# Theta's whole turns taken off by TensorE for the first two units, and a new order of steps

## The chip, the cores and the metric

The kernel runs on one core of a Trainium2 chip, in one launch. The metric is the time of one execution on the device, in microseconds, as the median of several runs; of the kernel before there are three, from 584.65 to 585.68, with a median of 585.23.

## The reference

Three stages over B = 4 batches of S = 768 tokens and 8 heads of 48 channels (384 together); all is float32.

```python
state = zeros((B, H, D, D))
for t in range(S):                       # 1: attention with a decaying state
    state = alpha[:, :, t, :, None] * state + einsum('bhd,bhe->bhde', k[:, :, t], v[:, :, t])
    y[:, :, t] = einsum('bhd,bhde->bhe', q[:, :, t], state)
x = y as (B, S, 384)
theta = x @ w_theta                      # 2: first mixer
z = einsum('ts,bsd->btd', w_tok_r, x * cos(theta)) + einsum('ts,bsd->btd', w_tok_i, x * sin(theta))
u = x + z
x = u + maximum(u @ w_ch, 0)
h = maximum(x @ w_in, 0); u, v = halves of h      # 3: second mixer, d_ff = 1024
v_n = (v - mean(v)) / sqrt(var(v) + 1e-6)
out = (u * (einsum('ts,bsd->btd', w_spatial, v_n) + b_spatial)) @ w_out
```

## The kernel before, in words

**Units.** The first two stages run over 24 units: unit u is batch u // 6 and a block of 128 tokens, u % 6. A unit's work is cut into steps, each a small function that issues its instructions on one engine:

- loads on SP's queue: load_al, load_qk, load_v; load_cst once (identity and mask)
- attention: att_scan (VectorE, three instructions: running products of the decays), att_qk (VectorE, q and k times the decays), att_a (TensorE, scores), att_mask for two halves (VectorE), move_a (SP: one half of the masked scores moved to the other partitions, through a tile "ay"), att_k (TensorE, four transposes of k), att_kt (ScalarE copies them), att_u (TensorE, update of the state), att_t and att_s (VectorE: state summed, then decayed, for two chunks c), att_y (TensorE, output), att_x (ScalarE copies it to x). From unit 6 on att_uy does att_u of the next unit and att_y together.
- first mixer: tr_p (TensorE, three transposes of x), tr_t and tr_h (ScalarE copies), tr_l (VectorE, the rest that tr_h's rounding leaves), th_p part 0 (six products with w_theta) and part 1 (three), th_k (ScalarE: theta in turns plus a magic constant, which rounds it to whole turns), th_r (VectorE: whole turns minus theta, into r), th_a (ScalarE: absolute value), th_s 0 and 1 (ScalarE: cosine and sine), z_m (VectorE: x times both), z_h and z_l (ScalarE, VectorE: split in two parts), tokmix for three blocks m and two of cos/sin (TensorE). Unit 0 is mixed in plain fp32 from whole tiles (line 610, tiles wf and zs), all others in three fp32r products of split parts.
- at a batch's end evac, ch_h, ch_l, ch_p, ch_e, ch_d: the channel product and the store of x to DRAM.

**Weights.** They come as 64-bit pieces: raw_f64 n loads one piece (on POOL's queue for n < 16, on SP's beyond) into one of two raw buffers, top n (ScalarE) and join n (VectorE) make a float32 of it, high n (ScalarE) and low n (VectorE) split that into two fp32r parts. Pieces 0 and 1 are w_theta, 2 to 13 the token weights, 14 and 15 w_ch. A load waits until join has read the buffer.

**The second mixer** runs batch by batch behind this: v_p, v_r, v_b, v_w, v_n, v_h, v_l; g_u and g_r; for batch 0 g_s, for the others seven block products g_p; g_b or g_c, g_m, g_h, g_l; o_p, o_e, o_d.

**Order.** Every step is registered once, with its engine and what it needs, and then issued in the order of the list ORDER (line 78 on), which holds the steps' numbers. Each engine executes its own steps in that order, as does SP's queue, so a step that waits holds up all behind it on its engine. The fields of `step` (cost, due time) play no part in the execution.

**Buffers that matter here.** PSUM has five accumulator banks and a pool "ps" of three banks. Theta of a unit (tile th), the transposes, the outputs y, and from unit 3 on the scores and k take turns in that pool. The SBUF buffers: al two, qk three, vd two (load_v), raw two.

**Lines named in the rows:** 342 load_al, 347 load_qk, 352 load_v, 357 to 361 att_scan, 369 att_qk, 383 att_a, 391 att_mask, 401 move_a, 407 att_k, 424 att_u, 434 att_s, 447 att_t, 466 att_y, 239 top, 248 join, 259 high, 267 low, 494 tr_p, 501 tr_h, 519 tr_l, 534 and 537 th_p, 541 th_k, 551 th_r, 572 z_m of unit 0, 610 tokmix.

Of the kernel before, what the change touches and what calls it, by code (L numbers as in the profile page):

```python
# [62 lines left out]
THP = ()  # L63
# [15 lines left out]
129 0 163 130 164 66 131 6 165 132 133 67 138 68 134 139 167 166 11 69 140 7 141 70 202 135 8 137 168 1 9 203 136 12 142 169 10 176 173 13 170 16 174  # L79
205 143 172 175 144 2 145 177 171 178 147 3 240 241 179 36 4 204 206 180 146 148 5 17 211 214 18 149 212 243 21 181 207 37 150 244 182 151 213 183 208  # L80
184 209 249 210 152 185 153 186 215 242 155 38 154 187 250 216 41 156 39 278 245 22 217 157 40 188 247 23 161 252 24 26 246 189 248 218 25 190 192 159
279 281 191 280 219 42 251 220 160 222 253 43 193 162 76 44 254 221 45 316 27 224 317 255 194 223 28 225 256 282 29 31 158 257 195 77 30 226 283 227
198 78 230 284 46 228 319 258 286 196 260 259 318 79 200 287 199 288 261 80 32 290 289 285 320 229 201 14 291 231 325 262 33 232 292 326 71 263 233
353 34 197 391 293 264 35 47 321 265 238 323 266 328 268 322 294 15 267 324 269 327 295 355 239 48 354 270 329 296 49 51 271 236 298 297 72 300 330 50
299 390 19 73 331 356 56 74 301 392 332 276 333 277 334 75 302 335 237 303 336 304 357 337 52 306 234 53 393 61 358 338 274 339 305 235 360 340 394
362 341 272 54 359 363 307 361 57 395 20 273 308 465 55 275 397 309 364 396 343 365 399 58 342 427 314 400 366 59 344 367 62 60 310 401 428 368 63 398
315 402 64 403 430 464 345 369 81 312 370 429 371 91 373 372 313 346 374 65 311 375 431 349 404 376 432 467 379 350 377 378 436 351 437 433 1015 405
435 468 347 406 466 434 380 82 407 348 438 408 439 409 440 381 473 410 501 352 441 474 502 1014 411 382 469 389 1016 412 383 470 413 414 385 504 415
417 442 1017 387 443 503 471 505 539 472 384 475 476 510 477 444 511 478 538 388 1018 446 445 416 386 447 83 506 1019 512 86 508 418 507 419 448 1020
509 420 479 541 421 575 480 540 423 513 514 449 515 574 425 542 450 1021 549 451 452 481 1022 424 482 453 484 483 543 454 1023 544 545 546 455 485 577  # L90
456 422 486 547 1024 487 426 548 1025 488 457 489 516 1026 578 462 576 517 1027 611 518 583 550 520 463 551 584 610 491 460 519 490 521 579 458 581
492 552 580 493 613 582 522 553 612 648 459 585 586 647 523 494 1030 524 525 614 526 461 528 527 619 529 499 620 554 555 530 557 1031 556 495 1032 650
558 1028 496 1029 1033 559 531 1034 615 560 497 617 561 651 562 587 563 616 564 621 500 588 649 565 685 622 589 566 532 623 624 684 591 658 590 618
656 592 593 657 652 536 653 654 655 687 498 594 625 595 567 534 722 626 659 596 533 660 721 661 627 688 686 535 628 597 630 629 631 695 599 598 693
570 724 694 689 632 571 633 691 634 537 690 635 600 87 662 725 601 568 602 723 663 692 696 664 569 697 665 795 698 666 1037 637 572 636 1036 726 667
573 727 609 729 728 668 638 758 605 639 640 730 603 731 1038 699 761 1039 606 760 759 669 732 607 670 700 671 604 674 733 734 701 735 794 608 1040 702
703 672 705 673 675 645 704 676 1043 762 797 767 768 646 706 707 1045 1044 708 677 709 1041 769 710 711 682 1042 712 763 713 641 765 764 714 766 736
798 643 1046 737 770 738 771 683 740 830 739 796 1048 799 801 741 1047 831 642 800 1049 802 719 833 644 803 742 804 678 772 743 832 868 720 744 773
745 679 748 805 834 867 746 1052 747 749 774 806 680 750 1053 776 835 775 681 777 751 778 837 836 870 838 839 779 756 780 840 1050 781 784 782 807
1051 783 785 1054 808 905 869 841 842 843 809 1055 717 904 810 871 1056 786 715 844 878 812 813 787 718 907 814 876 815 754 877 811 716 908 845 816  # L100
752 906 846 942 817 879 755 880 818 881 941 819 872 847 820 849 757 874 821 848 822 753 873 851 850 875 944 790 909 852 911 791 853 854 913 910 855
792 915 912 914 1059 882 945 788 883 979 916 884 917 789 885 918 978 886 887 857 793 1058 946 829 888 947 1060 949 950 825 981 943 889 823 890 856 827
891 951 858 892 1061 824 982 859 860 919 828 826 1062 980 920 948 861 84 85 921 862 923 952 922 893 953 865 924 894 954 955 983 895 925 984 896 985 88
863 89 101 926 864 92 90 927 897 987 1067 93 989 102 104 928 898 1068 988 931 103 866 107 1063 105 902 929 106 930 900 1064 110 932 986 899 933 956
934 1065 957 990 991 958 903 960 959 111 961 962 112 901 1066 113 963 1069 937 964 965 992 966 108 939 993 109 1070 1109 935 96 1071 994 114 940 995
115 967 1072 968 116 969 1074 1073 970 996 971 1076 1075 998 1077 997 1078 936 999 938 1000 1001 976 1002 1003 1035 972 974 1004 117 1005 118 1006 977
97 119 1007 975 94 1012 95 98 973 1112 124 1010 1114 1113 1013 1008 1081 1011 1115 1009 1080 1057 1116 1079 1091 1082 1123 1092 1117 1118 1097 1124
1119 99 1125 1093 1100 1083 1126 1130 1120 1098 1121 100 1095 1094 1122 1084 1127 1131 1101 1128 1088 120 1085 1096 1129 1086 1099 1132 1106 1089 1133
1087 1104 1107 1090 121 1102 1134 122 1105 125 1110 1137 123 1135 126 1136 1181 127 1138 1139 1144 1103 1140 1108 1141 128 1160 1145 1142 1146 1214
1111 1151 1161 1234 1147 1224 1148 1143 1149 1158 1152 1153 1167 1159 1150 1154 1155 1156 1174 1157 1162 1235 1236 1238 1169 1163 1164 1215 1165 1168  # L110
1237 1195 1216 1170 1166 1171 1176 1225 1175 1220 1226 1218 1188 1177 1178 1182 1183 1228 1179 1172 1180 1244 1229 1202 1184 1245 1190 1185 1186 1230
# [13 lines left out]
1580 1582 1581 1619 1583 1592 1620 1648 1585 1593 1586 1625 1641 1594 1595 1587 1596 1588 1589 1626 1590 1597 1621 1598 1655 1601 1649 1602 1599 1675  # L125
1600 1622 1623 1657 1624 1643 1627 1632 1659 1633 1628 1629 1636 1644 1660 1642 1630 1645 1650 1631 1646 1668 1651 1647 1637 1634 1656 1652 1661 1635
1658 1638 1639 1666 1653 1640 1676 1662 1654 1677 1667 1663 1664 1670 1669 1665 1678 1679 1684 1671 1680 1672 1682 1673 1674 1685 1689 1681 1683 1686
1687 1688 1692 1690 1691 1695 1693 1694 1698 1696 1697 1701 1699 1700 1704 1702 1703 1705 1706
""".split()]


# [1304 lines left out]
```

## Time and profile before

| | |
|---|---|
| median of three runs | 585.23 us |
| the profiled execution | 585.29 us |
| its span | 583.5 us |
| TensorE busy | 561.5 us, 96% |
| VectorE busy | 440.3 us, 75% |
| ScalarE busy | 252.5 us, 43% |
| GpSimd busy | 25.1 us, 4% |
| moved by DMA | 66.23 MB |

The span runs from the first to the last instruction of the program. In the rows PE is TensorE, DVE is VectorE, ACT is ScalarE, POOL is GpSimd and SP is SyncE, which issues most loads and stores; L551 is line 551 of the kernel. A row in order of time begins with the start and the duration in us; a number in brackets at its end is the engine's idle time before the instruction, and what ended it. An fp32 matmul shows as two records. Matmuls are pipelined: a duration reaches into that of the next one, so what a step costs is read from the distance of starts, or from a merged row of several.

### The profile page before, as it was taken

What the parts mean: (1) busy time and instruction counts of PE and PEld (TensorE: products, weight loads), DVE (VectorE), ACT (ScalarE), POOL (GpSimd) and SP (SyncE); (2) the same over time, 40 slices, a digit from 0 to 9 for tenths busy, and PEclk for the clock granted to TensorE, in tenths of its full rate; (3) what the DMA queues carried; (4) which work ended last, traced back from release to release, by engine and by line L of the source; (5) the groups of instructions that cost most, each with busy time, mean ns of one, the idle gap of its engine ahead of it and who ended that gap; (6) DMA issues with size and microseconds to landing.
All of it is one profiled execution on the core that took longest, in us unless ns stands there. A gap on an engine that the chain in (4) does not pass through costs nothing.

```text
span 583.5 us, 13445 instructions
## 1 busy us (share of the span) xinstructions
PE 561.5 (96%) x5737; PEld 510.4 (87%) x5737; DVE 440.3 (75%) x769; ACT 252.5 (43%) x474; POOL 25.1 (4%) x45
## 2 busy tenths in 40 slices
PE   1799999999999999999999999999999999999997
PEld 1666878888988889988989899999999899989997
DVE  6999999988788876878756887776665775767470
ACT  2476755435335433334554443534323441343232
POOL 1101100000000000000000100000000100011000
PEclk9999999999999999999999999999999999999999
DMA  8878756363253324333344525001002010211002
GB/s 287 295 240 278 245 184 215 112 198 126 86 169 110 104 88 128 122 104 97 95 139 168 180 89 183 1 0 62 20 2 95 29 41 0 82 42 40 1 1 81
DMA packets 28220, 66.23 MB, mean 114 GB/s; under 512 B 3073, under 2 KB 14337, under 8 KB 27905
## 3 DMA queue, kind: packets, MB, share of 16 engines
q1 hardware_dynamic: 25984, 53.51, 27.7%
q0 software_dynamic: 2176, 11.86, 5.9%
q8 instruction: 45, 0.74, 0.5%
q14 instruction: 15, 0.11, 0.1%
HBM read 52.78 MB, written 9.44 MB: 107 GB/s over the span
## 4 chain that ended last, share of the span: by engine, by line
PE 79%; DVE 10%; DMA 4%; ACT 2%; issue 2%; POOL 1%; DVEq 0%; SPq 0%; POOLq 0%; ACTq 0%
PE acc L610 22%; PE acc L929 11%; PE pu L861 8%; PE psc L652 7%; PE po L987 7%; PE psv L788 6%; PE sp L900 4%; PE th L534 3%; PE psuy L466 3%; DMA raw<-in_w 3%; PE th L537 2%; PE psa L383 2%; PE psuy L424 2%; PE psk L407 1%; DVE wf L248 1%
## 5 line engine op out<-in xcount | busy, mean ns | idle before, releaser
L610 PE MATMUL acc<-w,zs 128*128 128x256 f32 (+1 forms) x828 | 165.2, 344 | 0.0
L610 PEld LDWEIGHTS acc<-w,zs 128*128 128x128 f32 x828 | 128.0, 188 | 15.4
L788 PE MATMUL psv<-w,xs 128*128 128x512 f32 x216 | 53.7, 395 | 0.0
L987 PE MATMUL po<-w,gs 128*128 128x384 f32 x288 | 52.8, 338 | 0.3 <-ACT v L799 0.3
L861 PE MATMUL pu<-xs,w 128*128 128x384 f32 x288 | 53.0, 336 | 0.0
L987 PEld LDWEIGHTS po<-w,gs 128*128 128x128 f32 x288 | 50.7, 188 | 1.6 <-ACT v L799 0.7
L861 PEld LDWEIGHTS pu<-xs,w 128*128 128x128 f32 x288 | 50.3, 188 | 0.7 <-ACT o L997 0.2
L788 PEld LDWEIGHTS psv<-w,xs 128*128 128x128 f32 x216 | 40.0, 187 | 8.2 <-ACT v L799 0.2
L652 PE MATMUL psc<-us,wch 128*128 128x384 f32 (+1 forms) x243 | 41.2, 320 | 0.0
L652 PEld LDWEIGHTS psc<-us,wch 128*128 128x128 f32 x243 | 37.8, 189 | 0.8
L541 ACT ACTIVATE kk<-th,magic 128x384 f32<-128x384 f32 x24 | 13.9, 578 | 53.3 <-PE th L537 53.3
L973 ACT CAST gs<-t 128x384 fp32r<-128x384 f32 x32 | 15.8, 513 | 48.3 <-DVE t L966 48.3
L811 POOL TENSOR_TENSOR rs<-rs,mhalf 128x1 f32<-128x1 f32 x24 | 15.6, 652 | 441.7 <-DVE rs L808 441.7
L357 DVE TENSOR_TENSOR_SCAN al<-al,heads 112x536 f32<-112x536 f32 x24 | 30.5, 1270 | 3.3 <-DMA al<-in_al 3.3
L534 PE MATMUL th<-wth,xh 128*128 128x384 f32 x144 | 31.1, 352 | 0.9 <-ACT xh L501 0.5
L361 DVE TENSOR_TENSOR_SCAN al<-al,heads 112x536 f32<-112x536 f32 x24 | 30.6, 1275 | 0.8
L369 DVE TENSOR_TENSOR qk<-qk,al 112x1024 f32<-112x1024 f32 x24 | 29.3, 1220 | 2.1 <-DMA qk<-in_qk 2.1
L929 PE MATMUL acc<-w,mx 128*128 128x384 f32 x162 | 30.7, 338 | 0.0
L929 PE MATMUL acc<-wt,vns 128*128 128x384 f32 x162 | 30.7, 338 | 0.0
L929 PEld LDWEIGHTS acc<-wt,vns 128*128 128x128 f32 x162 | 28.6, 188 | 0.1
L929 PEld LDWEIGHTS acc<-w,mx 128*128 128x128 f32 x162 | 28.6, 188 | 0.0
L534 PEld LDWEIGHTS th<-wth,xh 128*128 128x128 f32 x144 | 25.4, 194 | 2.6 <-ACT xh L501 2.0
(122 smaller groups left out, 977.5 us busy)
## 6 DMA issues: line engine op xcount, KB each, us to landing
qk<-in_qk SPq DMA_DIRECT2D x24, 512.0 KB, 4.7
raw<-in_w POOLq DMA_DIRECT2D x14, 772.0 KB, 6.4
vd<-in_v SPq DMA_DIRECT2D x24, 288.0 KB, 4.0
al<-in_al SPq DMA_DIRECT2D x24, 268.0 KB, 3.3
raw<-in_w SPq DMA_DIRECT2D x6, 772.0 KB, 5.5
out<-o SPq DMA_DIRECT2D x24, 192.0 KB, 1.8
x2d<-xT SPq DMA_DIRECT2D x6, 576.0 KB, 4.4
ay<-ax SPq DMA_DIRECT2D x48, 64.0 KB, 2.8
```

Source lines behind the costliest of these rows:

```text
L357: nc.vector.tensor_tensor_scan(out=back[:, ::-1], data0=line[:, ::-1], data1=one[:, ::-1], initial=1.0, op0=ALU.mult, op1=ALU.add)
L361: nc.vector.tensor_tensor_scan(out=line, data0=line, data1=one, initial=0.0, op0=ALU.mult, op1=ALU.add)
L369: nc.vector.tensor_tensor(out=x, in0=x, in1=st[u]["ar"], op=ALU.mult)
L466: nc.tensor.matmul(psy[par][64 * c:64 * c + 64, a, :], w, v, start=part == 0 or first, stop=part == 1,)
L534: nc.tensor.matmul(th, xh[:, 0, k], wth[:, pr, k], start=(k == 0 and pr == 0), stop=False)
L610: nc.tensor.matmul(acc[b, n][:, c0:c1], zs[:, pl, ri, m * 128:(m + 1) * 128], w[:, pr, t0:t1], start=first and n != 1, stop=last, skip_gro ...
L652: nc.tensor.matmul(ps, wch[:, pl, k, m * 128:(m + 1) * 128], us[:, pr, k], start=(n == 0), stop=(n == 3 * KD - 1),)
L788: nc.tensor.matmul(ps, xs2[:, pl, k, o:o + 128], win[pr, "v"][:, k], start=(n == 0), stop=(n == 3 * KD - 1),)
L861: nc.tensor.matmul(pu, win[f // 2][:, pl, k * 256 + f % 2 * 128:k * 256 + f % 2 * 128 + 128], xq[b, h][:, pr, k], start=(n == 0), stop=(n ...
L900: nc.tensor.matmul(sp[:, :TH], vns[b, s][:, pl, f * 128:(f + 1) * 128], wsp[s][:, pr, t], start=(n == 0), stop=(n == 3 * NS - 1),)
L929: nc.tensor.matmul(g, left(b, n, j, pl, c), right(n, j, pr), start=(n in (1, 5, 6) and i == 0), stop=(i == 3 * NJ - 1), skip_group_check=n ...
L987: nc.tensor.matmul(po, gs[b][:, pl, f, s * 128:(s + 1) * 128], wo[f // 2][:, pr, f % 2 * DM:(f % 2 + 1) * DM], start=(n == 0), stop=(n == ...
```

## The change

One setting and the order differ.

THP = (0, 1) instead of an empty tuple. With it, for units 0 and 1, th_r goes, and two steps stand in its place: th_n (ScalarE) takes the magic constant off kk, which leaves the whole turns, and th_m (TensorE) multiplies them by a negative identity and adds that to theta in its PSUM bank. th_a and th_s 1 then read theta from that bank, not r. A step negate (ScalarE) makes the negative identity, 128x128, from the identity of load_cst. The functions were in the kernel before, unused.

```diff
-THP = ()
+THP = (0,1)
 STP = ()
...
-129 0 163 130 164 66 131 6 165 132 133 67 138 68 134 139 167 166 11 69 140 7 141 70 202 135 8 137 168 1 9 203 136 12 142 169 10 176 173 13 170 16 174
...
+130 131 67 165 166 7 0 132 167 168 133 134 68 135 69 169 12 8 139 70 140 141 137 136 71 138 142 170 205 206 9 171 143 2 10 178 13 11 175 173 1 172 14
...
```

The whole list is replaced; as the new steps are numbered in between, equal numbers don't mean equal steps. Decoded, by engine, the first steps read (unit or piece behind the name; att_mask, att_s, att_t with unit and half or chunk; th_p with unit and part; tokmix with unit, m and cos/sin):

```
PE before: att_k 0, att_a 0, att_u 0, att_a 1, att_k 1, att_y 0, att_u 1, tr_p 0, att_y 1, att_k 2, th_p 0 0, att_a 2, th_p 0 1, tr_p 1,
  att_u 2, att_k 3, th_p 1 0, th_p 1 1, att_a 3, tokmix 0 0 0, tokmix 0 2 0, att_y 2, tokmix 0 1 0, att_u 3, tr_p 2
PE after:  att_a 0, att_k 0, att_u 0, att_a 1, att_k 1, att_u 1, att_y 0, tr_p 0, att_y 1, att_k 2, th_p 0 0, th_p 0 1, tr_p 1, att_a 2,
  att_u 2, th_m 0, att_k 3, th_p 1 0, th_p 1 1, att_a 3, tokmix 0 0 0, th_m 1, att_y 2, tokmix 0 1 0, att_u 3, tokmix 0 2 0, tr_p 2
DVE before: att_scan 0, att_qk 0, join 13, att_scan 1, att_s 0 1, low 13, att_mask 0 0, join 1, att_qk 1, att_mask 0 1, att_t 0 1, low 1,
  att_s 1 0, join 2, att_mask 1 0, att_scan 2, att_t 1 0, att_mask 1 1, att_s 1 1, join 0, att_t 1 1, att_qk 2, tr_l 0, low 0, att_s 2 0,
  join 3, att_scan 3, att_qk 3, att_mask 2 0, att_mask 2 1, th_r 0, tr_l 1, att_t 2 0, join 7, att_s 2 1, z_m 0
DVE after: att_scan 0, att_qk 0, join 13, att_scan 1, att_mask 0 1, att_mask 0 0, low 13, att_s 0 1, att_qk 1, join 1, att_t 0 1, att_s 1 0,
  low 1, att_mask 1 1, att_mask 1 0, join 2, att_scan 2, att_t 1 0, att_s 1 1, att_qk 2, join 0, att_t 1 1, tr_l 0, att_s 2 0, low 0,
  join 3, att_scan 3, att_qk 3, tr_l 1, att_t 2 0, att_mask 2 0, att_s 2 1, join 7, z_m 0
ACT before: top 13, att_kt 0, high 13, top 1, high 1, top 2, att_kt 1, att_x 0, top 0, tr_t 0, high 0, tr_h 0, top 3, att_kt 2, att_x 1,
  top 7, th_k 0, tr_h 1, tr_t 1, th_a 0, th_s 0 1, th_s 0 0, att_kt 3
ACT after: top 13, top 1, high 13, att_kt 0, high 1, top 2, negate, att_kt 1, att_x 0, top 0, tr_h 0, tr_t 0, high 0, top 3, att_x 1, att_kt 2,
  th_k 0, tr_t 1, th_n 0, tr_h 1, top 7, th_a 0, th_s 0 1, th_s 0 0, att_kt 3
SP before: al 0, cst, qk 0, al 1, v 0, qk 1, v 1, al 2, move_a 0, qk 2, move_a 1, al 3, qk 3, v 2, move_a 2, v 3
SP after:  al 0, qk 0, al 1, cst, v 0, qk 1, v 1, move_a 0, al 2, qk 2, move_a 1, v 2, al 3, qk 3, v 3, move_a 2
```

POOL's queue of weight loads is the same in both (13, 1, 2, 0, 3, 7, 4, 8, 5, 15, 6, 9, 14, 10, 11, 12). Further on the same kind of changes goes through the whole list: token mixes of neighbouring units change places, some loads (qk 6, v 7, al 9, pieces 16 and 18) move by a few places in SP's queue, and in the second mixer some g_u, g_p, o_p and v_p change places. VectorE executes the same steps up to z_l 6, but for th_r 0 and 1. The last four steps of TensorE are the same.

## Rows read from the trace of the kernel before

**Rows 1.** The page, engines: busy us, share, instructions.
```profile
PE 561.5 (96%) x5737; PEld 510.4 (87%) x5737; DVE 440.3 (75%) x769; ACT 252.5 (43%) x474; POOL 25.1 (4%) x45
```

**Rows 2.** Windows: stretch, length, busy by engine (instructions), PEclk, DMA share, GB/s.
```profile
0.00:20.00 20.00, 5.72 (x110) 4.69 (x110) 15.41 (x27) 6.37 (x9) 3.70 (x10) 1.00 0.81 276
20.00:40.00 20.00, 17.80 (x280) 14.20 (x283) 18.41 (x32) 12.18 (x22) 2.01 (x4) 1.00 0.81 274
...
60.00:80.00 20.00, 19.85 (x296) 16.98 (x295) 19.00 (x29) 14.90 (x27) 2.11 (x4) 1.00 0.70 242
80.00:100.00 20.00, 19.30 (x267) 16.28 (x266) 19.86 (x31) 11.27 (x20) 0.00 (x0) 1.00 0.65 223
...
560.00:583.50 23.50, 20.18 (x115) 19.82 (x113) 7.55 (x15) 6.32 (x14) 0.00 (x0) 1.00 0.14 51
```

**Rows 3.** TensorE in order of time, 27 to 37 us: start, duration, instruction.
```profile
27.44 1.01 PE L407 MATMUL acc<-cst_sb,qk 112*128 112x112 f32 x4
28.12 2.27 PE L534 MATMUL th<-wth,xh 128*128 128x384 f32 x6
30.32 1.13 PE L383 MATMUL acc<-qk 48*64 48x64 f32 x32
...
33.13 0.60 PE L407 MATMUL psk<-cst_sb,qk 112*128 112x112 f32 x4
34.07 1.29 PE L534 MATMUL th<-wth,xh 128*128 128x384 f32 x6 [0.33 <-DVE r L551]
35.20 0.69 PE L537 MATMUL th<-wth,xh 128*128 128x384 f32 x3
35.82 0.76 PE L383 MATMUL psa<-qk 48*64 48x64 f32 x32
```

**Rows 4.** VectorE in order of time, 8 to 72 us.
```profile
9.73 0.96 DVE L248 SCALAR_TENSOR_TENSOR wf<-raw,zeros 128x768 uint32<-128x768 uint32 x1
...
22.48 0.36 DVE L447 TENSOR_TENSOR tmp<-acc,ss 112x192 f32<-112x192 f32 x1 [0.75 <-PE acc L424]
...
28.14 1.27 DVE L357 TENSOR_TENSOR_SCAN al<-al,heads 112x536 f32<-112x536 f32 x1
...
33.37 0.56 DVE L551 SCALAR_TENSOR_TENSOR r<-kk,th 128x384 f32<-128x384 f32 x1 [0.48 <-ACT kk L541]
...
35.99 0.95 DVE L572 SCALAR_TENSOR_TENSOR zs<-z,x 128x768 f32<-128x768 f32 x1
36.85 0.35 DVE L447 TENSOR_TENSOR tmp<-acc,ss 112x192 f32<-112x192 f32 x1
...
41.45 1.27 DVE L357 TENSOR_TENSOR_SCAN al<-al,heads 112x536 f32<-112x536 f32 x1 [0.24 <-DMA al<-in_al]
...
70.39 0.96 DVE L248 SCALAR_TENSOR_TENSOR wf<-raw,zeros 128x768 uint32<-128x768 uint32 x1 [0.86 <-ACT zeros L239]
```

**Rows 5.** ScalarE in order of time, 30 to 46 us.
```profile
31.83 1.08 ACT L239 ACTIVATE zeros<-raw 128x768 f16<-128x768 bf16 x1 [2.38 <-DMA raw<-in_w]
32.78 0.55 ACT L541 ACTIVATE kk<-th,magic 128x384 f32<-128x384 f32 x1
```

**Rows 6.** All engines in order of time, 30 to 45 us, a TensorE row.
```profile
36.99 2.85 PE L610 MATMUL acc<-wf,zs 128*128 128x512 f32 x8 [0.42 <-DVE zs L572]
```

**Rows 7.** Waits of TensorE: line, for whom; us in total, times, longest.
```profile
PE psy L466 <- DMA ay<-ax: 2.1, 3, 0.9
...
PE th L534 <- ACT xh L501: 0.5, 1, 0.5
```

**Rows 8.** SP's queue in order of time: start and duration of an issue.
```profile
13.70 0.33 SPq L342 DMA_DIRECT2D al<-in_al  x1
14.90 1.19 SPq L401 DMA_DIRECT2D ay<-ax  x2
16.13 0.59 SPq L347 DMA_DIRECT2D qk<-in_qk  x1
```

**Rows 9.** The page, DMA issues: count, KB each, median us to landing.
```profile
al<-in_al SPq DMA_DIRECT2D x24, 268.0 KB, 3.3
```

98 rows, old and new, of the table ORDER are left out of this document.

## The prediction

> **What bounds the kernel now.** I read the engine shares first, then the windows, then the early stretch of each engine in order of time. TensorE is busy 561.5 of 583.5 us [rows 1]. In the windows the first 20 us hold 5.72 us of TensorE work; from 20 us on it is nearly full: 17.80 of 20, then 19.85 and 19.30 [rows 2]. VectorE stands beside it: 18.41, 19.00 and 19.86 of 20 us. So until about 105 us two engines are full together, and afterwards TensorE alone. What is lost lies early: 14.3 us idle in the first window, 2.2 in the second, 0.85 between 60 and 80 and between 80 and 100 together, and 3.3 us in the last window, behind the last matmul and around it. Whatever moves the moment from which TensorE runs without gaps moves the end by the same amount, since the work behind it stays.
>
> There is a second early loss that "busy" hides. The four transposes of a K step take 1.01 us at 27.44 and 0.60 at 33.13, and the six first products of theta 2.27 us at 28.12 and 1.29 at 34.07 [rows 3]. The windows give a granted clock of 1.00 throughout, yet these durations say that TensorE ran at the lower of its levels (1.2 GHz) up to about 31 us and at 2.4 GHz after. Ahead of the change of level it had been busy since about 26 us without a gap.
>
> The run of this profile took 585.29 us, 1.8 more than its span; the median is 585.23, so the two can be used as one.
>
> **The change part by part.**
>
> *Theta of units 0 and 1.* Removed: two th_r on VectorE, 0.56 us each [rows 4]. A VectorE instruction starts about 0.09 us before the one ahead of it ends (35.99 for 0.95, next start 36.85), so each is worth 0.47, together 0.95 us of VectorE's time. Added on ScalarE: two th_n, priced as th_k, 0.55 us each [rows 5], and one negate of 128x128, between 0 and 0.55, taken as 0.3. ScalarE is 60 to 75% busy there (12.18 of 20, 14.90 of 20 [rows 2]), so its time costs nothing as such; only its order can. Added on TensorE: two th_m, fp32 with 384 columns. There is no such row. Nearest is the first token mix: 8 records, which are four fp32 matmuls of 512, 256, 512 and 256 columns, in 2.85 us [rows 6]; half of these 1536 columns' time for 768 is 1.42, so 0.71 for 384. The lower end is one of the three fp32r matmuls of 384 columns that took 0.69 together [rows 3], 0.23; the upper end is twice 0.71 at the lower clock. I take 0.71 each, +1.42 us of TensorE for both, as it is the same kind of operand.
>
> *What waits for them.* th_n and th_m stand between th_k and the sines, so the chain of unit 0 gets 0.55 + 0.71 instead of 0.56, about 0.7 longer. The theta bank of units 0 and 1 is now held until the sine has read it instead of until th_r, one of three rotating PSUM buffers. Behind it on TensorE stands att_a 3, which needs two of them; it needs att_kt 3 on ScalarE, as it does now. On ScalarE top 7 now stands ahead of th_a 0 and waits for a load; that wait was 2.38 us before [rows 5], ahead of th_k 0. Cost: between 0 and +1; taken as 0, since in the new order tr_t, th_n and tr_h fill that time.
>
> *VectorE's order until 50 us.* Up to z_l 6 it executes the same steps as before without two th_r, so its clock can be followed by its gaps. load_qk 0 now goes out ahead of load_cst, one issue (some 0.4 us) earlier, but join 13 at 9.73 [rows 4] follows ScalarE's top 13 and so the weights' load, not qk: 0. At 22.48 VectorE waits 0.75 us for att_u 1, which TensorE executes behind att_y 0, which in turn waits for the landing of ay (2.1 us of such waits in all [rows 7]). Now att_u 1 is ahead of att_y 0, and move_a 0 is ahead of load_al 2 in SP's queue. The 0.75 goes; next late is att_a 1's result at the second mask of unit 1, by some 0.1. I take -0.6, which puts scan 3 at 27.5 instead of 28.14. The wait of 0.48 at 33.37 goes with th_r, but tr_l 1 then waits for tr_h 1, now behind th_n 0 on ScalarE: from -0.5 to +0.7, taken as 0. The 0.24 at 41.45 goes too, as att_s 2 1, which frees that buffer, comes before join 7: -0.2. Sum for VectorE: -0.95 - 0.6 - 0.2 = -1.75 us.
>
> *SP's queue.* load_al 2 was issued at 13.70, when att_s 0 1 had freed its buffer; move_a 0 at 14.90 and load_qk 2 at 16.13 followed [rows 8]. Now the masks come first, move_a 0 at about 14.2, and att_s 0 1 behind low 13, so load_al 2 goes out at about 15.2 and qk 2 at 15.7. At 3.3 us per such load [rows 9] al lands at 18.5, and scan 2 wants it at 19.5: covered by 1 us, and each us beyond that is a us of VectorE. Weight loads 0 and 3 go out 0.9 to 1.3 later, as join 1 and join 2 move back on VectorE; join 0 is moved behind att_qk 2, which covers it. Later moves in this queue (load_qk 6, load_v 7, the late weight pieces) I cost from -0.5 to +1, at 0: the wire has room from 60 us on.
>
> *TensorE until 50 us.* th_p 0 0 wants low 0, which comes 0.3 us earlier, and att_y 1, which no longer ends at 27.4 but about a us sooner, as ay 1 and att_s 1 1 are there before: -1.0. att_a 2 (1.13 us at the lower clock against 0.76 at 35.82 [rows 3]) moves behind the change of level: -0.4. The gaps of 0.33 ahead of 34.07, 0.42 ahead of 36.99 and 0.5 ahead of the theta of unit 2 [rows 3, 6, 7] are filled by the th_m: -1.25. Added +1.42. Sum: -1.23 us. TensorE's is the later of the two sums and decides: -1.2.
>
> *From 50 to 112 us* VectorE is full with one gap of 0.86 at 70.39 [rows 4], and TensorE loses what VectorE's order makes it wait. VectorE enters this stretch 0.5 us further ahead than TensorE. I take -0.5, the bounds being 0 and -3 (the gaps of both). *Behind 112 us* TensorE is full in both; the reordered products of the second mixer can gain or lose some tenths: 0. The last steps are the same.
>
> Sum: 585.29 - 1.2 - 0.5 = 583.6 us.
>
> The clock is where a page speaks against the change. Rows 3 show the level rising after a stretch without gaps. The Trainium skill ("TensorE: Matmul & The Clock Gate", What's actually happening) says that the throttled state is the default and that activity releases it; the trace agrees with the doubled durations before 31 us. By the rule a TensorE that waits at 26 to 27 us, as the new order may make it, would get its level later; that is the second rival below.
>
> **The rivals.**
>
> *The gaps close altogether.* VectorE loses also the 0.86 and TensorE its small waits up to 112 us: another 2 to 2.5 us, 581.3 us. For it: both engines have the same work and are full for 97%. Against: the waits are many and small, each for another step.
>
> *The level rises later.* If the new order leaves TensorE idle ahead of th_p 0 0 and the rise comes at 34.5 instead of 31 us, then 3.5 us of its time do half the work, which costs 1.75: 585.3 us, no change. For it: low 0 is only 0.3 us earlier and att_y 1 a whole us, so a gap of that size opens there. Against: att_y 1 has gaps of that size now.
>
> *The products find no gap* (slower). Between 31 and 112 us TensorE is full for 97 to 99%; if the new order only moves its waits, as VectorE's order is as tight as before, the 1.42 us of the two th_m come on top: 586.7 us. It decides for slower once less than 0.25 us of the waits go. For it: the page's rows show TensorE as the engine that ends last, and work is moved to it from one that is free after 105 us. Against: VectorE is as full in just the stretch where the products stand.
>
> **How the numbers follow.** Forecast 0.45, with its own range from 582.4 to 584.4; gaps close 0.17; later level 0.20; no gap 0.18. 0.2% is 1.17 us, about what a measurement of this kernel can tell from no change. Faster by more (below 584.1): most of the forecast and the first rival, 0.58; within it 0.25; slower (above 586.4) 0.17. The range reaches from 581.0 to 586.4: the first rival's value inside, most of the last one's outside.
>
> **What would show it.** VectorE: no gap ahead of att_t 1 0, scan 3 near 27.5, no th_r before unit 2's. TensorE: two fp32 products on theta of some 0.7 us, the first theta product near 27 us, the first token mix near 36. A K step's transposes at 0.60 us by 33 us. The forecast is wrong if the first gapless stretch of TensorE begins no earlier than now, if ScalarE's top 7 holds th_a 0 back, or if al 2 lands after VectorE asks for it.

## The result, and the profile after

The change makes the kernel slower: 588.03 us median of seven executions (587.36 to 591.43) against 585.27 (584.65 to 586.1, seven) for the kernel before, ratio 1.0055, interval 1.0033 to 1.0077. The forecast was 583.6, with a range from 581.0 to 586.4.

The profiled execution took 591.43 us (span 589.3). It is the slowest of the seven, 3.4 us above their median, so not all that it shows is paid each time; the experiments below tell for a part of it whether it is. Its engines, and its windows as in [rows 1, 2]:

```profile
PE 564.9 (96%) x5741; PEld 512.1 (87%) x5741; DVE 440.8 (75%) x767; ACT 255.6 (43%) x477; POOL 25.7 (4%) x45
```
```profile
0.00:20.00 20.00, 5.73 (x122) 4.57 (x126) 14.94 (x28) 6.46 (x10) 3.17 (x9) 1.00 0.78 265
20.00:40.00 20.00, 17.35 (x284) 14.13 (x276) 17.68 (x28) 12.98 (x24) 2.12 (x4) 1.00 0.78 264
40.00:60.00 20.00, 17.93 (x240) 12.98 (x241) 17.02 (x25) 11.48 (x23) 1.63 (x4) 0.91 0.75 255
60.00:80.00 20.00, 20.00 (x329) 17.16 (x328) 19.09 (x31) 15.51 (x29) 2.08 (x4) 1.00 0.79 246
80.00:100.00 20.00, 19.46 (x240) 16.55 (x239) 19.39 (x30) 12.38 (x21) 0.53 (x1) 1.00 0.57 199
```

The stretch to look at is 40 to 60 us, where a granted clock of 0.91 stands. From 60 to 80 us TensorE is without a gap, where it lost 0.15 before. TensorE around 40 us in order of time, against [rows 3, 6]:

```profile
28.87 2.27 PE L534 MATMUL th<-wth,xh 128*128 128x384 f32 x6
...
33.86 0.91 PE L547 MATMUL th<-kk,negative 128*128 128x384 f32 x2
34.61 0.55 PE L407 MATMUL psk<-cst_sb,qk 112*128 112x112 f32 x4
...
37.42 1.56 PE L610 MATMUL acc<-wf,zs 128*128 128x512 f32 x4
38.82 0.81 PE L547 MATMUL th<-kk,negative 128*128 128x384 f32 x2
39.56 0.33 PE L466 MATMUL psy<-ss,qk 48*64 48x48 f32 x8
39.71 0.28 PE L466 MATMUL psy<-vd,ay 64*64 64x48 f32 x2
42.07 0.27 PE L466 MATMUL psy<-vd,ay 64*64 64x48 f32 x3 [2.09 <-DMA ay<-ax]
...
43.03 2.78 PE L610 MATMUL acc<-wf,zs 128*128 128x256 f32 x4
```

The two products on theta have the size that was forecast: from start to the next start 0.75 and 0.74 us. But att_y 2 stops for 2.09 us in the middle, for the moved half of its scores, and the token mix behind it, four records, takes 2.78 where the four at 37.42 take 1.56. The windows show why:

```profile
40.00:42.00 2.00, 0.00 (x0) 0.00 (x0) 0.84 (x2) 0.15 (x1) 0.53 (x1) 1.00 1.00 331
42.00:44.00 2.00, 1.93 (x57) 1.70 (x58) 1.22 (x1) 0.86 (x3) 0.00 (x0) 0.80 1.05 346
44.00:46.00 2.00, 2.00 (x15) 0.50 (x15) 1.93 (x4) 1.97 (x4) 0.00 (x0) 0.50 0.91 369
46.00:48.00 2.00, 2.00 (x36) 1.44 (x31) 1.59 (x3) 0.36 (x1) 0.00 (x0) 0.84 0.27 102
```

TensorE idles from 40 to 42 us, and then the granted clock falls back to the lower level (1.2 GHz): 0.80, 0.50, 0.84 in the next three windows, at 1.2 us of extra duration for that one mix. The Trainium skill ("TensorE: Matmul & The Clock Gate", What's actually happening) calls the throttled state the default, which activity releases. The trace agrees: it shows the way back to that state behind a wait. VectorE's and SP's rows tell where the 2.09 come from, first VectorE, against [rows 4], then SP's queue, against [rows 8]:

```profile
31.57 1.23 DVE L369 TENSOR_TENSOR qk<-qk,al 112x1024 f32<-112x1024 f32 x1
34.17 0.56 DVE L519 TENSOR_TENSOR xh<-pst,xh 128x384 fp32r<-128x384 f32 x1 [1.38 <-ACT xh L501]
34.65 0.35 DVE L447 TENSOR_TENSOR tmp<-acc,ss 112x192 f32<-112x192 f32 x1
34.91 0.41 DVE L391 TENSOR_TENSOR ax<-acc,cst_sb 128x256 f32<-128x256 f32 x1
...
42.78 1.27 DVE L357 TENSOR_TENSOR_SCAN al<-al,heads 112x536 f32<-112x536 f32 x1 [1.94 <-DMA al<-in_al]
```
```profile
35.35 2.07 SPq L401 DMA_DIRECT2D ay<-ax  x2
37.51 0.54 SPq L342 DMA_DIRECT2D al<-in_al  x1
```

The rows of before for the same two steps:

```profile
34.12 0.56 DVE L519 TENSOR_TENSOR xh<-pst,xh 128x384 fp32r<-128x384 f32 x1 [0.20 <-ACT xT L506]
```
```profile
32.58 1.11 SPq L401 DMA_DIRECT2D ay<-ax  x2
```

tr_l 1 waits 1.38 us for tr_h 1, which on ScalarE now stands behind tr_t 1 and th_n 0; att_mask 2 0 stands behind tr_l 1, and move_a 2 needs that mask. So the move goes out at 35.35 and lands at 42.03; before it stood ahead, went out at 32.58 and landed at 35.15. That is 6.9 us later, and the issue makes only 2.8 of them: from the start of the first issue to the landing it takes 6.7 us here and 2.6 before. The load of al 4 stands behind move_a 2 in SP's queue, goes out at 37.51, lands at 42.76, and att_scan 4 waits 1.94 for it. All this belongs to that execution: in early_new's, with the same order up to 115 us (see the experiments), neither tr_l 1 nor TensorE waits there, and the move, out at 32.53, lands at 35.82.

```profile
31.36 0.55 DVE L526 TENSOR_TENSOR xh<-pst,xh 128x384 fp32r<-128x384 f32 x1
```
```profile
32.53 1.81 SPq L408 DMA_DIRECT2D ay<-ax  x2
```

In the trace after, TensorE's waits for ay, 2.1 us in all before [rows 7], come to twice that, about half of it here and half at att_y 1 (in us: total, times, longest):

```profile
PE psy L466 <- DMA ay<-ax: 4.1, 2, 2.1
```

How the whole time is divided is best read as a lag: at moments when TensorE has executed the same set of steps in both kernels, the start of its next step, this kernel's minus that of before (start times from the two traces; us):

```
moment in before      27.4   43.1   53.5   84.7  112.0  137.1  264.6  298.9  337.9  497.4  562.5
after                +0.75  +5.03  +3.69  +2.64  +3.77  +3.63  +4.73  +5.73  +6.65  +5.97  +5.89
order_only           -1.56  +0.03  +1.02  -0.30  +2.00  +1.86  +2.21  +3.17  +3.51  +2.80  +2.70
early_new            -1.76  -0.43  -0.83  -1.53  -0.72     (order of before from 115 us on)
rest_new             (order of before up to 115 us)     -0.26  +0.93  +1.93  +2.50  +1.79  +1.69
rest_k21             (order of before up to 115 us)     -0.60  -0.22  +0.84  +2.01  +1.31  +1.21
after_mend           -1.00  +0.54  -0.06  -1.40  -0.70  -0.86  -0.52  +0.90  +1.27  +0.57  +0.47
```

(The names are those of the experiments.) Two things are to be seen. The early part differs from one profiled execution to the next by several us, though after and early_new issue the same instructions up to 115 us; what all four with the new early order share is a loss of 0.7 us or more between 84.7 and 112 us. And from 137 to 338 us every kernel with the new order loses 1.7 to 3.0 us, of which it wins 0.8 back by 562 us. The forecast had put this stretch at 0.

### The profile page after: what moved, and what is told of

It reads as the page before. It is cut to its first block, busy times and chain, and to the rows that moved or that the text cites. A ratio compares the mean times of both kernels' runs of the same rounds, so it can differ in the third digit from the quotient of the medians.

```text
span 589.3 us, 13465 instructions
## 1 busy us (share of the span) xinstructions
PE 564.9 (96%) x5741; PEld 512.1 (87%) x5741; DVE 440.8 (75%) x767; ACT 255.6 (43%) x477; POOL 25.7 (4%) x45
## 4 chain that ended last, share of the span: by engine, by line
PE 71%; DVE 11%; DMA 4%; issue 2%; ACT 2%; POOL 0%; DVEq 0%; ACTq 0%; POOLq 0%
PE acc L610 15%; PE acc L929 11%; PE pu L861 8%; PE po L987 8%; PE psv L788 7%; PE psc L652 6%; PE sp L900 4%; PE th L534 3%; DMA al<-in_al 3%; PE psuy L466 2%; PE th L537 1%; PE psuy L424 1%; PE psa L383 1%; DVE al L357 1%; DVE qk L369 1%
## 5 line engine op out<-in xcount | busy, mean ns | idle before, releaser
L239 ACT ACTIVATE zeros<-raw 128x768 f16<-128x768 bf16 (+1 forms) x22 | 22.9, 1041 | 11.5 <-DMA raw<-in_w 8.8
```

The costliest lines, as they stand in the source:

```text
L239: nc.scalar.activation(out, c["top"].rearrange("p (c k) -> p c k", k=4)[:, :, 0], AF.Identity, scale=0.5)
```

## The experiments

All were timed beside the kernel before, whose median stands in each table; the ratios are with 95% intervals. Orders are put together at cut points: "up to X" means the list up to that step, then what is left in the other list's order. In the rows of experiments the line numbers are 7 higher than in those of before and after (th_m is L554).

### The change divided

thp_only has the order of before with the products, order_only the new order without them; early_new takes the whole change up to att_uy 8 (about 115 us), rest_new the new order from there on.

```diff
thp_only:    -THP = ()    +THP = (0,1)    ORDER: -th_r u  +th_n u, th_m u   (u = 0, 1)   +negate behind load_cst
order_only:   THP = ()    ORDER: the new one, -th_n u, th_m u  +th_r u;  -negate
early_new:   +THP = (0,1) ORDER: the new one up to att_uy 8, then the old
rest_new:     THP = ()    ORDER: the old one up to att_uy 8, then the new
```

> The order of before, with THP = (0,1): negate behind load_cst, th_n and th_m where th_r stood. Theory W (the new order's waits cost the time: some early, about half between 112 and 350 us): the two products fall mostly into gaps, 585.3 to 586.1 us. Theory P (the two products are the loss): 586.7 to 588 us.

> The new order, but THP empty: th_r where th_m stood, no negate and no th_n. Theory W: 587 to 588 us, nearly all of the loss. Theory P: 585 to 586 us, nearly none.

> THP = (0,1) and the new order up to att_uy 8 (about 117 us), then the order of before. Theory W: 585 to 586.2 us in most executions, as the lag of some 3.8 us that the profile after shows at 117 us belongs to an execution in which the clock fell after unit 2's outputs waited; some executions with that fall 2 to 4 us longer. Theory P: 586.7 to 588 us, as for the products alone.

> THP empty, the order of before up to att_uy 8 (about 113 us), then the new order. Theory W: 586.8 to 588 us, since the profile after falls 2.7 us further behind between 117 and 350 us and regains 0.7 later. Theory P: 585 to 585.8 us.

| | median | before | ratio |
|---|---|---|---|
| thp_only | 589.04 | 585.8 | 1.0050 [1.0034, 1.0067] |
| order_only | 588.41 | 585.8 | 1.0039 [1.0024, 1.0054] |
| early_new | 587.33 | 585.8 | 1.0022 [1.0010, 1.0035] |
| rest_new | 586.87 | 585.8 | 1.0019 [1.0005, 1.0033] |

Both parts cost by themselves, and both halves of the list do. Neither theory held as a whole: rest_new came out as theory W has it, order_only 0.4 us above W's range, early_new in P's range and thp_only above both. The halves add up to 0.41%, between order_only and the change; products and order don't add up (0.50 + 0.39%), so the products must be dearer in the old order than in the new. ScalarE of thp_only, in order of time, shows how:

```profile
28.08 0.55 ACT L489 COPY x<-psy 128x192 f32<-128x192 f32 x2
35.27 1.07 ACT L246 ACTIVATE zeros<-raw 128x768 f16<-128x768 bf16 x1 [6.64 <-DMA raw<-in_w]
36.21 0.56 ACT L548 ACTIVATE kk<-th,magic 128x384 f32<-128x384 f32 x1
```

There top 7 still stands ahead of th_k 0 and waits 6.64 us for its load. TensorE first waits 2.41 us for load_v 2, which lands late too in that execution, and then 0.96 for th_n 0, which th_m 0 wants; the granted clock of that execution was 0.50 in every 2 us from 30 to 40 us. In the kernel before the wait of top 7 was 2.38 [rows 5], VectorE's th_r was behind it, and TensorE lost 0.33 [rows 3].

early_new's profiled execution, at 585.1 us the fastest of its twelve, is the one in which the forecast for the early stretch can be checked undisturbed. TensorE and VectorE in order of time:

```profile
26.36 1.95 PE L541 MATMUL th<-wth,xh 128*128 128x384 f32 x6
...
31.50 0.60 PE L414 MATMUL psk<-cst_sb,qk 112*128 112x112 f32 x4 [0.20 <-DVE qk L376]
...
34.44 0.33 PE L390 MATMUL psa<-qk 48*64 48x64 f32 x4 [0.61 <-ACT z L573]
...
35.97 1.56 PE L617 MATMUL acc<-wf,zs 128*128 128x512 f32 x4
```
```profile
9.09 0.96 DVE L255 SCALAR_TENSOR_TENSOR wf<-raw,zeros 128x768 uint32<-128x768 uint32 x1 [1.49 <-ACT zeros L246]
...
27.37 1.27 DVE L364 TENSOR_TENSOR_SCAN al<-al,heads 112x536 f32<-112x536 f32 x1
```

scan 3 stands at 27.37 (forecast 27.5), the first theta product at 26.36 (27), the first mix at 35.97 (36), K's transposes at 0.60 by 31.5. att_a 3 waits 0.61 us for a sine of unit 0 (L573), which reads theta in the bank that att_a 3 takes next; that hold was named in the forecast and costed at nothing. Join 13, which in the new order waits for the first weight piece, starts at 9.09 here and at 10.16 after (at 9.73 before [rows 4]). So of the 2.51 us between early_new and after at 27.4 us, 1.07 are there when the first load has landed, with the same order in both; the rest comes at att_y 1, whose moved scores land 2.5 us later in after, at 26.47 instead of 23.96.

### The waits that the profiles name, one by one

```diff
thp_top7:   thp_only, ACT: -top 7, th_k 0 ... th_n 0   +th_k 0 ... th_n 0, top 7
early_fix:  early_new, DVE: -tr_l 1, att_t 2 0, att_mask 2 0  +att_mask 2 0, tr_l 1, att_t 2 0
                       SP:  -v 3, move_a 2  +move_a 2, v 3;   raw_f64 16 behind qk 8
rest_fix:   rest_new, DVE: att_scan 22 behind both masks of unit 21; att_t 22 0 ahead of join 17
tail_new:   THP = (), the old order up to tokmix 23 0 1 (about 326 us), then the new
```

> As thp_only (order of before with the two products; 589.04 us), but top 7, which waits for a weight load on ScalarE ahead of th_k 0, goes behind th_n 0. If the products cost what they make TensorE wait for (th_m 0 stands ahead of th_p 1 0 and waits for ScalarE's th_n 0), 586.3 to 587.6 us; if they cost their own time and a bank held longer, 588.5 to 589.5.

> As early_new (THP and the new order up to att_uy 8, then the order of before; 587.33 us), but att_mask 2 0 and with it move_a 2 go ahead of tr_l 1 and load_v 3, and raw_f64 16 goes behind load_al 8 and load_qk 8 in SP's queue. Theory Q (the new early order loses its gain to loads and moves that stand late in SP's queue: ay 2, al 4, al 8): 585.3 to 586.4 us, no scan 8 that waits over 0.3 us, no wait of att_y 2 for ay. Theory P (what is lost there is the two products): 587 to 588 us, unchanged.

> As rest_new (order of before up to att_uy 8, then the new one, THP empty; 586.87 us), but att_scan 22 goes behind both masks of unit 21, and att_t 22 0 ahead of join 17. Theory W: the waits of att_k 21 (0.92 us, for a mask behind a scan that waits for al) and att_a 23 (0.5 us, for att_t 22 0 behind a join that waits for a load) go, 585.5 to 586.3 us, and the lag against before at 346 us is about 1.4 instead of 2.5 us. If the loss there is spread over many waits of equal size instead, 586.6 to 587.2 us.

> The order of before up to the last token mix (326 us), then the new order, THP empty: only the second mixer is new. The profiles show the new order regaining 0.6 to 0.8 us there: 584.7 to 585.4 us against 585.8 (theory W). If that is no property of the order, 585.5 to 586.1.

| | median | before | ratio |
|---|---|---|---|
| thp_top7 | 586.06 | 585.45 | 1.0010 [0.9996, 1.0023] |
| early_fix | 587.16 | 585.45 | 1.0022 [1.0001, 1.0044] |
| rest_fix | 588.14 | 585.45 | 1.0045 [1.0025, 1.0065] |
| tail_new | 585.20 | 585.45 | 0.9991 [0.9974, 1.0007] |

thp_top7 settles the products in the old order: moving one ScalarE step takes 0.40% off, and its trace has top 7 behind th_n 0 with no wait. The two products themselves cost 0.10% there, about 0.6 us, which can't be told from nothing but is less than their 1.5 us of TensorE.

early_fix brought nothing. It put move_a 2 ahead, and no wait for ay is left; but att_scan 4 waited 2.57 us for al 4, and the lag went from +0.39 at 45 us to +3.47 at 53.5. al 4 didn't go out late, at 33.71 against 34.43 in early_new; it landed late, 7.3 us after that instead of 2.9. The traces show what it meets on the way: weight piece 8, which POOL's queue issues when join 7 is done. On VectorE join 7 stands close to att_s 2 1, which frees the buffer for al 4 (us from the span's start; landing from the start of the issue):

| | al 4 goes out | piece 8 goes out | al 4 takes to land | att_scan 4 waits |
|---|---|---|---|---|
| early_new | 34.43 | 34.96 | 2.91 | - |
| early_fix2 | 35.03 | 36.08 | 3.61 | - |
| after_mend | 33.60 | 34.66 | 4.31 | - |
| early_fix | 33.71 (to 35.11) | 34.21 | 7.33 | 2.57 |
| order_only | 35.82 | 35.60 | 5.66 | 1.53 |
| early_base | 35.93 | 35.47 | 5.38 | 1.57 |
| after | 37.51 | 36.75 | 5.25 | 1.94 |
| before | 36.10 | 36.35 | 5.33 | 0.24 |

Where the issue of al 4 is over when piece 8 goes out (in early_new to 0.01 us), it lands in 2.9 to 4.3 us; otherwise it takes 5.3 to 7.3 us and lands within 1.2 us of that piece. The second half of move_a 2 in after, whose issue ends at 37.42, behind the 36.75 of the piece, lands at 42.03, beside the piece's 41.78. So part of what differs between executions in the early stretch looks like a race of two loads, which the order of steps sets up. Eight traces agree on it; no run was made that moves piece 8 alone, so it isn't shown.

rest_fix was worse than rest_new: the wait of att_k 21 was gone (the distance from th_p 19 1 to it fell from 1.28 to 0.52 us), but the other edit, att_t 22 0 moved up, lengthened the steps around it (tokmix 19 1 1 from 1.15 to 1.82). From 137 to 338 us its trace loses 2.9 us where rest_new's loses 2.8, so the 0.26% between the two times isn't explained by that stretch. tail_new can't be told from no change, and its trace says why the 0.8 us behind 338 us are no gain: with nothing new ahead of 326 us its lag goes from -0.32 at 299 us to +0.30 at 338 and back to -0.37 at 497. The new tail wins back what it has lost itself.

### The early stretch mended, and the price of the products in the new order

```diff
early_fix2: early_new, DVE: -tr_l 1, att_t 2 0, att_mask 2 0, att_s 2 1  +att_mask 2 0, att_t 2 0, att_s 2 1, tr_l 1
                       SP:  -al 4 behind v 3, move_a 2   +move_a 2, al 4, v 3;   raw_f64 16 behind qk 8
early_base: early_new without the products (th_r 0 and 1 where th_m stood, no negate)
tail_top7:  tail_new, ACT: top 7 behind th_k 0
thp_tail:   thp_top7 up to tokmix 23 0 1, then the new order
```

> The order up to att_uy 8 (about 115 us) is the new one with the products, then that of before, as in early_new (+0.22%). One edit: on VectorE att_mask 2 0, att_t 2 0 and att_s 2 1 go ahead of tr_l 1, which waits for tr_h 1; on SP move_a 2 and load_al 4 go ahead of load_v 3; raw_f64 16 goes behind load_qk 8. Theory A (SP's queue and tr_l 1 hold ay 2 and al 4 back, so TensorE waits ahead of att_y 2, and its clock falls a second time): the wait of 2.1 us ahead of att_y 2 goes, ay 2 lands before 40.5, att_scan 4 waits under 0.6 us, time 0.2 to 0.35% below early_new: 585.3 to 586.2 where before has 585.5. Theory B (the early loss lies in the products and VectorE's tightness): the wait moves to another step and the time stays within 0.1% of early_new, about 587.

> The new order up to att_uy 8 without the products (th_r 0 and 1 on VectorE where th_n stood), then the order of before. With early_new this gives the price of the two products in the new order. Theory A (the early order costs, the products are small): 586.4 to 587.3 where before has 585.5, the products then +0 to +0.9. Theory B (the products cost their own 1.5 us and the early order nothing): 585.4 to 585.9.

> The order of before up to tokmix 23 0 1 (about 326 us), from there the new one, without the products, and on ScalarE top 7 behind th_k 0, so that the wait for raw 7 no longer holds theta of unit 0 back. Theory A (that wait is paid in every execution): th_a 0 starts up to 2 us earlier and the time is 584.3 to 585.2 where before has 585.5. Theory B (join 7 and VectorE are then late by as much): no change, 585.2 to 585.8.

> The order of before with the products for units 0 and 1, top 7 behind th_n 0 on ScalarE, and from tokmix 23 0 1 on (about 326 us) the new order. If the parts add (thp_top7 +0.10%, tail_new -0.09%): 585.2 to 586.0 where before has 585.5. If the products cost their own time whatever the order: 586.5 to 587.

| | median | before | ratio |
|---|---|---|---|
| early_fix2 | 586.36 | 585.37 | 1.0014 [0.9997, 1.0031] |
| early_base | 587.03 | 585.37 | 1.0027 [1.0008, 1.0047] |
| tail_top7 | 585.40 | 585.37 | 0.9991 [0.9975, 1.0007] |
| thp_tail | 586.05 | 585.37 | 1.0015 [1.0000, 1.0031] |

early_base says that the early loss is there without the products: the early order costs 0.27% without them (th_r in their place) and 0.22% with them. Each of the two numbers has a margin of 0.1 to 0.2%, so a price of the products below 1 us or so stays possible. early_fix2 did what its edit was for: the second half of move_a 2 lands at 36.65, al 4 at 38.64, and no wait for ay is left. Its time is 0.08% under early_new, within the noise, where the first theory wanted 0.2 to 0.35%; the second theory's "within 0.1%" is what was met, though not its 587 us, and early_base speaks against the first of its reasons, the products. Its profiled execution, at 588.36 the slowest of its twelve, starts late (join 13 at 10.46) and has a lag of +2.18 at 43.1 us; then it shows what came in place of the wait, TensorE in order of time:

```profile
43.71 0.59 PE L617 MATMUL acc<-wf,zs 128*128 128x256 f32 x2
45.27 0.55 PE L501 MATMUL pst<-cst_sb,x 128*128 128x128 f32 x3 [0.97 <-ACT kk L563]
```

tr_p 2 waits 0.97 us for th_a of unit 1 (L563), which with the products reads theta in its bank, and tr_p 2 takes that bank next. The same row shows 0.5 us in early_fix and 0.7 in after_mend, and is in none of the kernels without the products. Those have another in its place, att_y 3 waiting for tr_l's result on VectorE (the waits of TensorE between 36 and 60 us, early_base):

```profile
PE psy L473 <- DVE xh L526: 1.0, 1, 1.0
```

With the products it is 0.3, but for 1.1 in early_fix. So in most of these traces the products move about as much wait from VectorE's side to ScalarE's as they take.

tail_top7 shows no gain from top 7 in the kernel without products; its theory A falls. Both kernels with the new tail alone end at 0.9991, under the kernel before by less than can be told; of all that were run they are the only ones not above it. thp_tail, at 0.15%, is above the sum of its parts (0.01%), which its interval just holds, and below what the products' own 1.5 us would add (0.26%), which the interval doesn't exclude.

### The middle divided

What was open by then is the loss between 137 and 338 us.

```diff
mid1:        THP = (), the old order, but the new from att_uy 8 to tokmix 17 2 1 (115 to 265 us)
mid2:        THP = (), the old order, but the new from tokmix 17 2 1 to tokmix 23 0 1 (265 to 326 us)
rest_k21:    rest_new, DVE: att_scan 22 behind both masks of unit 21
after_mend:  the change, with the edits of early_fix2 and of rest_k21
```

> The order of before, but for the stretch behind att_uy 8 (about 115 us) up to tokmix 17 2 1 (about 265 us), which is in the new order; no products. In the profile of rest_new TensorE's lag against before went from about -0.7 at 137 us to +0.9 at 265. Theory A (the loss behind 115 us is spread over the units, small waits everywhere): +0.10 to +0.20%, 586.0 to 586.6 where before has 585.4. Theory B (it lies in a few waits of the last units, behind 250 us): 585.2 to 585.8.

> The order of before, but for the stretch from tokmix 17 2 1 (about 265 us) to tokmix 23 0 1 (about 326 us), which is in the new order; no products. Lag in rest_new over this stretch: +0.9 to +2.5. Theory A (spread): +0.10 to +0.25%, 586.0 to 586.9. Theory B (the late load of al 22, which is issued ahead of this stretch, makes most of it): 585.3 to 585.9, and no wait of att_scan 22.

> rest_new (+0.19%) with one edit: on VectorE att_scan 22 goes behind both masks of unit 21, so that the wait for al 22 no longer holds att_k 21 back. If that wait is a loss of the end: the row of TensorE that waits 0.9 for the mask goes, and the time falls by 0.5 to 0.9 us, to about 586.0 where before has 585.4. If other waits take its place, as they did in rest_fix: 586.5 to 587.

> The changed kernel (+0.55%) with the two edits together: those of early_fix2 (att_mask 2 0, att_t 2 0 and att_s 2 1 ahead of tr_l 1, move_a 2 and load_al 4 ahead of load_v 3, raw_f64 16 behind load_qk 8) and that of rest_k21 (att_scan 22 behind the masks of unit 21). If both waits are paid at the end: 586.2 to 587.3 where before has 585.4, +0.15 to +0.35%. If the time is lost elsewhere: 587.8 to 588.6, no better than the changed kernel.

| | median | before | ratio |
|---|---|---|---|
| mid1 | 588.14 | 585.85 | 1.0036 [1.0022, 1.0050] |
| mid2 | 587.32 | 585.85 | 1.0021 [1.0009, 1.0033] |
| rest_k21 | 587.60 | 585.85 | 1.0020 [1.0003, 1.0037] |
| after_mend | 587.37 | 585.85 | 1.0022 [1.0003, 1.0041] |

Both stretches lose by themselves, mid1 more than expected by either theory: lag -0.42 at 137.1 us and +2.77 at 266; mid2 +2.04 at 331, in time within its theory A (+0.10 to +0.25%). Most of mid1's is the seam back to the old order: the lag is +0.83 at 259.4 us and 1.9 us more by 266.

The lags also say where the loss lies, and it isn't spread over the units. From 137 to 259 us order_only, rest_k21 and after_mend lose 0.2 to 0.3 us, rest_new and after 1.0 to 1.1, most of it in the one wait shown below. From 259 to 299 us every trace with the new order there loses again, 1.1 to 1.6 us (2.2 in rest_fix). Two steps on TensorE make most of that. att_a 23 takes 1.12 us to the next start instead of 0.62 in all but mid2 (1.40 in rest_fix), as its second part waits for att_t 22 0 on VectorE; and tokmix 18 0 0, the first of batch 3's mix, takes 0.2 to 0.9 us longer, as its second part waits for VectorE to clear an accumulator. One row of each, of rest_k21 and of after_mend:

```profile
281.26 0.68 PE L390 MATMUL psa<-qk 48*64 48x64 f32 x28 [0.18 <-DVE tmp L454]
```
```profile
266.36 2.12 PE L617 MATMUL acc<-w,zs 128*128 128x256 f32 x11 [0.37 <-DVE acc L626]
```

The wait ahead of 259 us is this one, VectorE of rest_new, then what it does on TensorE:

```profile
256.63 1.27 DVE L364 TENSOR_TENSOR_SCAN al<-al,heads 112x536 f32<-112x536 f32 x1 [0.92 <-DMA al<-in_al]
...
259.37 0.40 DVE L398 TENSOR_TENSOR am<-psa,cst_sb 128x256 f32<-128x256 f32 x1
```
```profile
258.54 0.68 PE L544 MATMUL th<-wth,xh 128*128 128x384 f32 x3
259.83 0.60 PE L414 MATMUL psk<-cst_sb,qk 112*128 112x112 f32 x4 [0.60 <-DVE am L398]
```

al 22 is issued at 251.46 instead of 249.22 and lands late; the masks of unit 21 stand behind the scan, and att_k 21 behind them. rest_k21 takes that away: the row is gone and the lag at 264.6 us is -0.22 instead of +0.93 (0.34 of the difference is there at 137 us already). And yet the time is that of rest_new. The trace says where it went: by 338 us the lag is +2.01, and TensorE has this row, which before has not,

```profile
325.88 2.13 PE L617 MATMUL acc<-w,zs 128*128 128x256 f32 x11 [0.54 <-DVE xT L631]
```

a mix of the last unit that waits until VectorE has added a finished accumulator to x (evac); that step stands behind one of the second mixer, which waits 1.21 us for ScalarE. In this trace an earlier TensorE only waits longer at the next place.

after_mend is 0.22% above before where the change was 0.55%, as expected by the theory that the named waits are paid; since rest_k21 gave nothing, this is put down to the early edit, whose own run gave 0.08%. The intervals of the two are wide enough to hold one value near 0.2%, but that the early edit gains isn't shown.

## Why the prediction was wrong

**The step that failed outright** is "*Behind 112 us* TensorE is full in both ...: 0". It took TensorE's full windows as proof that the order there is free. The five traces of the lag table that have the new order there lose 1.7 to 3.0 us between 137 and 338 us and win back 0.8; by time rest_new is 0.19% (1.1 us) slower. Step by step, each step's distance to the next start less the same in before, rest_new's 2.8 us are 1.6 in four steps that are 0.2 us or more longer (th_p 19 1 by 0.66, att_a 23 by 0.50, ch_p 3 1 1 by 0.24, att_uy 19 by 0.22) and 1.15 in differences below 0.2 each. The two largest wait for VectorE. The windows hardly show it: from 137 to 338 us TensorE is busy 201.00 us of 201 before and 200.15 in rest_new, so of the 2.8 us only 0.85 count as idle.

**"TensorE until 50 us: -1.2" and "From 50 to 112 us: -0.5"** were nearly met in one execution, the fastest of early_new (lag -0.43 at 43.1, -0.83 at 53.5, -1.53 at 84.7 us), with each of its marks within 0.7 us; but also there the lag is back at -0.72 at 112 us, and in the median the same instructions make 0.22% (+1.3 us). Three terms failed. The gaps "filled by the th_m: -1.25" are gone in early_new, but others of 0.16, 0.20, 0.61 and 0.59 us stand there, so that of 1.76 us ahead at 27.4 us 0.43 are left at 43.1. "The 0.24 at 41.45 goes too ...: -0.2": att_scan 4 waited 1.94 us for al 4 in after, 1.53 in order_only and 1.57 in early_base. al 4 landed at 42.76, 41.48 and 41.31 there, no earlier than before (41.43), as it meets a weight load and, in after, stands behind a late move_a 2; the sum had no term for that, its "Later moves in this queue" name other loads. And tr_l 1's wait, "from -0.5 to +0.7, taken as 0", was 1.38 in the profile after (none in early_new); the text asked what is late on VectorE and not what stands behind tr_l 1: att_mask 2 0, and through it move_a 2, for which TensorE waited 2.09. From 106 to 112 us each of these kernels loses 0.7 to 0.8 in small waits, where the forecast had "the bounds being 0 and -3" from 50 us on. How much of these each execution pays, and so why the median of early_new is 1.3 above before although its fastest execution is not, stays open: early_fix2 and after_mend, with the waits for ay 2 and al 4 removed, are 0.08% (within the noise) and 0.33% faster than their parents.

By medians the two stretches account for the result: 583.6, and 3.0 us for an early gain of 1.7 that was a loss of 1.3, and 1.1 for the later stretch, make 587.7; 588.03 was measured.

**The rival "level rises later"** described a mechanism that the trace after shows in another place: a second fall, at 42 us, which cost 1.2 us in one mix of that execution. The first rise was late there too, but by about a us (an estimate from durations) and not to 34.5: three products of theta at 30.94 still take 1.16 us, the three at 28.14 in early_new 0.69. The fall isn't paid always: order_only and early_base show TensorE idle for about half of 2 us (1.04 of 2.00 busy from 38 to 40 us in early_base) with a granted clock of 1.00 behind it.

**"The products find no gap"** had the right sign and a price near the early kernels' (586.7), but the products aren't the main reason: order_only costs 0.39% without them. In the new order they cost -0.05% (early_new less early_base) to +0.16% (after less order_only), each with a margin of some 0.25%; in the old one 0.10%, and 0.50% where ScalarE's order was left as it was.

**What was right:** 0.71 us for a product (0.75 and 0.74); al 2 at 18.5 (it landed at 18.87, and the scan at 19.83 didn't wait); the wait of 0.86 at 70.39, gone; the danger of top 7 ahead of th_a, which cost nothing in the new order, as taken, and 0.40% in thp_only, where it stands ahead of th_k 0 too. The bank held by the sines was named and then costed at nothing, for att_a 3; it held att_a 3 by 0.61 us in early_new and tr_p 2 by 0.5 to 1.0 in the mended kernels.

## What to carry to other kernels

A step that gets a new wait is priced by what stands behind it on its engine and, one further, by the transfers that those steps issue: here, in one execution, a wait of 1.38 us on VectorE, with what was put ahead of the mask, sent a move out 2.8 us later, which then landed 6.9 us later, and TensorE and VectorE waited 2.09 and 1.94 us for DMA. So look also at what else is issued at that moment: by the traces a small load took 2.9 to 4.3 us when it was out ahead of a weight load, and 5.3 to 7.3 when not. A "full" engine in the windows isn't proof that the order there is free; take the distances between starts, step by step, before a reordering of a full stretch is costed at nothing. Where removing the largest named wait changes the lag there and not the end, as in rest_k21, look at which engine the next wait is for (here VectorE again).

## What had not been expected of the hardware

- The granted clock can fall again in the middle of a nearly full stretch: after 2.09 us of waiting it was 0.80 and 0.50 in the next two windows of 2 us, and the mix took 2.78 instead of 1.56 us.
- The second issue of move_a 2 took 1.55 us in the trace after (35.87 to 37.42; the first 0.47), against 0.59 before. Of the single issues of move_a in the first 140 us, before has 2 of 24 over 0.8 us, after 5 of 22. Some of the long ones lie beside an issue of a weight load on POOL (at 36.75 for 0.53 us here), some don't; the cause isn't settled, and no run was made for it.
- The same program varies by more than such a change is worth: the kernel before took from 583.73 to 589.17 us in the 35 executions beside early_base. With a dozen executions of a kernel the intervals still reach 0.12 to 0.22% to either side.
